# Fewer half slices beside the attention, three loads on ScalarE's queue, a shorter float64 conversion, and low weights on VectorE in every other step

## The chip, the cores and the metric

One core of one Trainium2 chip. The metric is device time in microseconds (us) of one launch. The tensor engine (TensorE, PE in the rows) multiplies; VectorE (DVE), ScalarE (ACT) and GpSimd (POOL) do elementwise work; SyncE (SP) issues most of the transfers (DMAs). Each engine works through its own instructions in order and waits on semaphores for the others. The kernel's matmuls are fp32, most of them as three products of a high and a low part.

## The reference

Three layers, one after the other, on 3072 tokens of 512 features:

```
state = gamma * state + k_t^T v_t;  y_t = scale * q_t state        # B=4, H=8, S=768, D=64
e = argmax(x w_gate); out = gate * sigmoid(x w_output_gate)[e] * relu(x w1[e]) w2[e]   # 8 experts, 512->1024->512
h = x w_in;  out = (h - tanh(h)) w_out                              # 512->2048->512
```

`w_in` and `w_out` come as float64; the kernel gets them as 64-bit words (`w64`) and makes two fp32 parts of each, high and low.

## The kernel before

The whole order of work is written out by hand; no scheduler moves anything.

**Attention** (`for n in range(NT - 1)`, lines 915 to 997). 24 tiles of 128 tokens, six for each batch element. A step loads a later tile (`load`, 1 MB of q, k, k, v), does `attend(n)` (state times q, state update, scores times v), `scores(n + 2)` (k times q, masked by VectorE into `pt`) and `rows(n)` (turns the tile, computes the gates' logits and stores the tokens to `xtok`). A tile's loads go five tiles ahead, later three. Six tile buffers are there up to step 18, then four. After 8, 16 and 24 tiles VectorE picks the expert of each token (`onehot`, `ranks`, `scale`, `slots`): the step's short VectorE instructions.

Beside it run half slices of the float64 weights. `load_m` brings one (128 x 512 words of 64 bits), `conv_m` makes its parts in three stages: `begin` (ScalarE), `v0` to `v5` (VectorE) and `high` (ScalarE), `rest` (GpSimd). For the last four slices of `w_in`/`w_out` (f of `NRES` and up) the parts stand in `keep` and `ta` and are stored to DRAM (`dh`, `dl`) until the dense layer; a later half slice takes the same `keep` buffer only when that store is done. `fill` gives VectorE instructions of `scales` and `convs` to a step until `MOST` = 2.6 us of estimated work are handed out; `pump` hands out those of ScalarE and GpSimd. At step `EARLIER` = 18 whatever is left of `convs` is issued at once, because its pool is given back.

**Experts** (`mm1`, `mm2`, lines 1001 to 1135). 72 steps of a 128-wide slice of one expert's hidden features: `mm1(i)` 12 matmuls, `mm2(i - 1)` 12 matmuls. `load_w` brings a slice (512 KB), `conv_w(i, 0)` and `conv_w(i, 1)` make its high part on ScalarE (line 236, `wh`) and its low part (line 238, `wl`): on GpSimd for part 0 (`mm1`'s weights), on VectorE for part 1 (`mm2`'s). Beside steps 14 to 66 the other 26 half slices are converted, one in two steps: stage 2 of one and stage 0 of the next in an even step, stage 1 in an odd one.

**Dense layer** (`mm3`, `mm4`, lines 1236 to 1262): six blocks of 512 tokens by 16 slices, 12 + 12 matmuls each.

What the change touches: `NPA`, `conv_w` (230), `conv_m` (263), `load` (589), the attention loop's loads and pieces (908 to 963), the end of the attention (1029 to 1042) and the loop over expert steps (1085 to 1126).

## Time and profile before

| | |
|---|---|
| time, median of 3 runs | 1042.34 us (1039.9 to 1042.95) |
| the profiled execution's own time | 1040.79 us |
| its span, first to last instruction | 1038.8 us |
| around the span | 2.0 us |
| busy in the span | PE 977.4, PE weight load 841.6, DVE 779.2, ACT 604.6, POOL 429.6 us |
| first matmul of the experts | 159.4 us |
| first matmul of the dense layer | 492.5 us |
| moved by DMA | 120.69 MB |

Times in rows are us from the start of the span. An instruction's row says its engine, line, operation and tiles (out<-in); in square brackets stands how long the engine was idle before it, and what ended that. The granted clock is TensorE's share of its full speed.

### The profile page before, as it was taken

What the parts mean: (1) busy time and instruction counts of PE and PEld (TensorE: products, weight loads), DVE (VectorE), ACT (ScalarE), POOL (GpSimd) and SP (SyncE); (2) the same over time, 40 slices, a digit from 0 to 9 for tenths busy, and PEclk for the clock granted to TensorE, in tenths of its full rate; (3) what the DMA queues carried; (4) which work ended last, traced back from release to release, by engine and by line L of the source; (5) the groups of instructions that cost most, each with busy time, mean ns of one, the idle gap of its engine ahead of it and who ended that gap; (6) DMA issues with size and microseconds to landing.
All of it is one profiled execution on the core that took longest, in us unless ns stands there. A gap on an engine that the chain in (4) does not pass through costs nothing.

```text
span 1038.8 us, 16501 instructions
## 1 busy us (share of the span) xinstructions
PE 977.4 (94%) x5938; PEld 841.6 (81%) x5938; DVE 779.2 (75%) x1183; ACT 604.6 (58%) x1090; POOL 429.6 (41%) x363
## 2 busy tenths in 40 slices
PE   7996676999999999999999999999999999999995
PEld 5875566999999999999888888888888888888884
DVE  2595765578989999994797777777777777777772
ACT  3433332265556565564786776677676667667662
POOL 4445341345645655644243352343324324323322
PEclk9998688999999999999999999999999999999998
DMA  9979361356757657664500010010001001000001
GB/s 333 345 280 362 127 208 62 112 190 208 213 163 244 202 179 232 199 189 154 204 21 21 1 61 11 11 41 22 19 11 52 11 11 51 11 0 21 21 1 43
DMA packets 44010, 120.69 MB, mean 116 GB/s; under 512 B 9638, under 2 KB 15014, under 8 KB 41106
## 3 DMA queue, kind: packets, MB, share of 16 engines
q1 hardware_dynamic: 35602, 100.38, 29.2%
q0 software_dynamic: 4864, 12.91, 3.8%
q10 hardware_dynamic: 3456, 6.29, 1.6%
q8 instruction: 48, 0.79, 0.3%
q14 instruction: 40, 0.33, 0.1%
HBM read 95.99 MB, written 23.57 MB: 115 GB/s over the span
## 4 chain that ended last, share of the span: by engine, by line
PE 66%; DVE 11%; DMA 10%; POOL 5%; issue 4%; ACT 2%; SPq 1%; POOLq 0%; ACTq 0%; DVEq 0%
PE mh L1194 26%; PE ma L1208 26%; PE ph L430 6%; PE ya L454 5%; DMA ld<-in_qkv 3%; POOL wl L238 3%; DMA wr<-in_w 2%; DVE wl L238 2%; DMA m<-in_w 1%; DVE ta L290 1%; ACT wh L236 1%; POOL ml L311 1%; DMA dh<-keep 1%; DVE ta L277 1%; DVE va L280 1%
## 5 line engine op out<-in xcount | busy, mean ns | idle before, releaser
L1176 POOL TENSOR_TENSOR gl<-g,gh 128x512 fp32r<-128x512 f32 x96 | 124.0, 1291 | 343.9 <-ACT gh L1175 327.6
L1194 PE MATMUL mh<-x2h,ml 128*128 128x512 f32 x384 | 151.7, 395 | 0.0
L1208 PE MATMUL ma<-ml,gh 128*128 128x512 f32 x384 | 151.6, 395 | 0.0
L1194 PE MATMUL mh<-x2h,mh 128*128 128x512 f32 x384 | 151.6, 395 | 0.0
L1208 PE MATMUL ma<-mh,gl 128*128 128x512 f32 x384 | 151.3, 394 | 0.0
L1208 PE MATMUL ma<-mh,gh 128*128 128x512 f32 x384 | 150.9, 393 | 0.0
L1194 PE MATMUL mh<-x2l,mh 128*128 128x512 f32 x384 | 150.9, 393 | 0.0
L1169 DVE COPY_PREDICATED g<-big,td 128x512 f32<-128x512 int32 x96 | 143.0, 1489 | 9.9
L1159 DVE SCALAR_TENSOR_TENSOR g<-s,mh 128x512 f32<-128x512 f32 x96 | 65.8, 686 | 101.8 <-ACT s L1157 87.1
L236 ACT ACTIVATE wh<-wr 128x512 fp32r<-128x512 f32 x136 | 84.3, 627 | 88.6 <-PE ya L454 75.9
L238 POOL TENSOR_TENSOR wl<-wr,wh 128x512 fp32r<-128x512 f32 x68 | 100.3, 1476 | 83.8 <-ACT wh L236 78.9
L1155 ACT ACTIVATE u<-mh 128x512 f32<-128x512 f32 x96 | 57.5, 599 | 128.2 <-PE mh L1194 123.6
L430 PE MATMUL ph<-xh,wl 128*128 128x216 f32 (+7 forms) x288 | 97.4, 338 | 5.9 <-POOL wl L238 5.5
L430 PE MATMUL ph<-xh,wh 128*128 128x216 f32 (+7 forms) x288 | 97.3, 338 | 0.1
L454 PE MATMUL ya<-lo,wh 128*128 128x216 f32 (+7 forms) x288 | 95.3, 331 | 0.7 <-DVE lo L434 0.7
L430 PE MATMUL ph<-xl,wh 128*128 128x216 f32 (+7 forms) x288 | 95.5, 332 | 0.3 <-DVE xl L410 0.3
L454 PE MATMUL ya<-hi,wh 128*128 128x216 f32 (+7 forms) x288 | 95.2, 331 | 0.0
L454 PE MATMUL ya<-hi,wl 128*128 128x216 f32 (+7 forms) x288 | 95.1, 330 | 0.0
L1194 PEld LDWEIGHTS mh<-x2l,mh 128*128 128x128 f32 x384 | 72.1, 188 | 17.2
L1194 PEld LDWEIGHTS mh<-x2h,ml 128*128 128x128 f32 x384 | 72.1, 188 | 17.2
L1208 PEld LDWEIGHTS ma<-mh,gh 128*128 128x128 f32 x384 | 72.1, 188 | 17.0
L1208 PEld LDWEIGHTS ma<-ml,gh 128*128 128x128 f32 x384 | 72.1, 188 | 17.0
(183 smaller groups left out, 2086.1 us busy)
## 6 DMA issues: line engine op xcount, KB each, us to landing
wr<-in_w SPq DMA_DIRECT2D x68, 512.0 KB, 5.2
ld<-in_qkv SPq DMA_DIRECT2D x22, 1024.0 KB, 13.5
m<-in_w SPq DMA_DIRECT2D x32, 512.0 KB, 5.0
xtok<-xr ACTq DMA_DIRECT2D x24, 256.0 KB, 7.4
...
```

Source lines behind the costliest of these rows:

```text
L236: nc.scalar.activation(hi, t[:, cs], AF.Copy)
L238: eng.tensor_tensor(out=lo, in0=t[:, cs], in1=f32(hi), op=ALU.subtract)
L277: V.tensor_scalar(mcv[j]["ta"], word(1), 5, 2, op0=ALU.logical_shift_left, op1=ALU.logical_shift_right)
L280: V.scalar_tensor_tensor(out=mcv[j]["va"], in0=word(1), scalar=0xC0000000, in1=mcv[j]["ta"], op0=ALU.bitwise_and, op1=ALU.bitwise_or,)
L430: nc.tensor.matmul(ph, a[:, cs], b[:, kk, 0:ns], start=(k == 0), stop=(k == 3 * KD - 1))
L454: nc.tensor.matmul(accs[p][dk], a[:, cs], b, start=(k == 0 and j == 0 and (p > 0 or dk % 2 == 0)), stop=(k == NFE - 1 and j == 2), skip_gr ...
L1155: nc.scalar.activation(u, h, AF.Square)
L1159: nc.vector.scalar_tensor_tensor(out=g, in0=s1, scalar=PB1, in1=h, op0=ALU.add, op1=ALU.mult)
L1169: nc.vector.copy_predicated(g, big.bitcast(I32), td)
L1176: nc.gpsimd.tensor_tensor(out=lo, in0=g, in1=f32(hi), op=ALU.subtract)
L1194: nc.tensor.matmul(h, a[:, cs], c, start=(k == 0), stop=(k == 3 * KD - 1))
L1208: nc.tensor.matmul(macc[b][t], a[:, cs], c[:, DM:2 * DM], start=(f == 0 and j == 0), stop=(f == NFM - 1 and j == 2))
```

## The change

1. `NPA` 6 to 4: two half slices less beside the attention (26 and 27 of 32), two more beside the experts. In the attention a further half slice is loaded only while fewer than two stand loaded and unused (`len(m64) < 2`).
2. `begin` multiplies the word by 2 to the minus 112 (`DOWN`) in place of squaring it (a copy with a scale); `v0` and `v1` read its result `keep`, not the word; `v5`, which zeroed tiny numbers, is gone.
3. Tile 2 is loaded ahead of `decay(2)` by SP, tiles 3 to 5 from ScalarE's queue.
4. The experts' first slices are loaded by `feed()` at the top of steps 15 and up, behind the tile's load, in place of `load_w()` at 13, 14, 15 and `feed()` at the end of a step.
5. At the end of the attention `run(sc[7:])` (17 short VectorE instructions) stands ahead of `mm1(2)`, and `slots` ahead of `conv_w(4, 1)`.
6. In the expert loop the low part 0 of odd steps is made by VectorE; that of even steps stays on GpSimd.
7. The 57 stages of the 28 remaining half slices are spread evenly over 53 steps.

```
@@ -53,7 +53,7 @@
 MOST = 2.6
 FAR = 1.0e6
 PG = P + 2 * E
-NPA = 6
+NPA = 4
 NRES = 12
 SCALE = 1.0 / float(D) ** 0.5
 
@@ -64,7 +64,8 @@
 PU = 0.36
 
 
-TINY = (1.125 * 2.0 ** -15) ** 2
+
+DOWN = 2.0 ** -112
 
 
 C_MASK = 0
@@ -227,14 +228,14 @@
         while state["load"] < min(len(loads), state["conv"] + 3):
             load_w()
 
-    def conv_w(i, part):
+    def conv_w(i, part, eng=None):
         t = raw[i]
         cs = slice(part * DM, (part + 1) * DM)
         pool = whl_p if i >= NFE or i % 4 < 2 else whl2_p
         hi = pool.tile([P, DM], F32R, tag=f"wh{part}", name=f"wh{part}_{i}", bufs=2)
         lo = pool.tile([P, DM], F32R, tag=f"wl{part}", name=f"wl{part}_{i}", bufs=2)
         nc.scalar.activation(hi, t[:, cs], AF.Copy)
-        eng = nc.vector if part else nc.gpsimd
+        eng = eng or (nc.vector if part else nc.gpsimd)
         eng.tensor_tensor(out=lo, in0=t[:, cs], in1=f32(hi), op=ALU.subtract)
         whl[i, part] = (hi, lo)
         if NFE // 2 <= i < NFE:
@@ -271,14 +272,14 @@
         def begin():
             t = {k: cv_p.tile([P, DM], U32, tag=k, name=f"{k}{j}", bufs=b) for k, b in cv_bufs[cv_p].items()}
             mcv[j] = t
-            nc.scalar.activation(f32(t["keep"]), f32(word(1)), AF.Square)
+            nc.scalar.activation(f32(t["keep"]), f32(word(1)), AF.Copy, scale=DOWN)
 
         def v0():
-            V.tensor_scalar(mcv[j]["ta"], word(1), 5, 2, op0=ALU.logical_shift_left, op1=ALU.logical_shift_right)
+            V.tensor_scalar(mcv[j]["ta"], mcv[j]["keep"], 4, 1, op0=ALU.logical_shift_left, op1=ALU.logical_shift_right)
 
         def v1():
             V.scalar_tensor_tensor(
-                out=mcv[j]["va"], in0=word(1), scalar=0xC0000000, in1=mcv[j]["ta"],
+                out=mcv[j]["va"], in0=mcv[j]["keep"], scalar=0x80000000, in1=mcv[j]["ta"],
                 op0=ALU.bitwise_and, op1=ALU.bitwise_or,
             )
 
@@ -293,10 +294,6 @@
         def v4():
             vf = f32(mcv[j]["va"])
             V.tensor_tensor(out=vf, in0=vf, in1=f32(mcv[j]["ta"]), op=ALU.add)
-
-        def v5():
-            vf = f32(mcv[j]["va"])
-            V.scalar_tensor_tensor(out=vf, in0=f32(mcv[j]["keep"]), scalar=TINY, in1=vf, op0=ALU.is_ge, op1=ALU.mult)
 
         def high():
             if f < NRES:
@@ -315,7 +312,7 @@
 
         return [
             [("A", begin), ("V", v0), ("V", v1), ("V", v2)],
-            [("V", v3), ("V", v4), ("V", v5)],
+            [("V", v3), ("V", v4)],
             [("A", high), ("P", rest)],
         ][stage]
 
@@ -586,7 +583,7 @@
                 cs = slice(hp * P, (hp + 1) * P)
                 nc.scalar.activation(qt[c][:, cs], qt[c - 1][:, cs], AF.Copy, scale=ca[:, C_STEP + hp:C_STEP + hp + 1])
 
-        def load(n):
+        def load(n, eng=nc.sync):
             if n < EARLIER and n % 6 >= 4:
                 t = ldb_p.tile([P, 4, DM], F32, tag="ld", name=f"ld{n}")
             else:
@@ -603,7 +600,7 @@
                 nc.sync.dma_start(t[:, 0:2], qkv[n, :, 0:2])
                 nc.sync.dma_start(t[:, 2:4], qkv[n, :, 2:4])
             else:
-                nc.sync.dma_start(t, qkv[n])
+                eng.dma_start(t, qkv[n])
             if n == 1:
                 nc.sync.dma_start(cb, conb)
                 nc.sync.dma_start(wgs, wg)
@@ -905,7 +902,9 @@
             nc.vector.tensor_copy(turn_rhs[:, kk, P:], wgs[:, kk])
         scores(1)
         nc.vector.tensor_copy(tri, cb[:, B_TRI:B_TRI + P])
-        nld = 2
+        load(2)
+        load(3, nc.scalar)
+        nld = 4
         decay(2)
         J0 = 2 * NFM - NPA
         convs, scales, soon, after = [], [], [], []
@@ -923,18 +922,18 @@
                 flush()
                 rooms()
             while nld < NT and nld <= n + (5 if nld < EARLIER + 4 else 3):
-                load(nld)
+                load(nld, nc.scalar if nld < 6 else nc.sync)
                 nld += 1
+            if n >= TA - 1:
+                feed()
             flush()
 
-            if n >= 2 and n % 2 == 0 and nload < NPA:
+            if n >= 2 and n % 2 == 0 and nload < NPA and len(m64) < 2:
                 load_m(J0 + nload, cva_p)
                 nload += 1
-            if n >= 4 and n % 2 == 0 and nconv < NPA:
+            if n >= 4 and n % 2 == 0 and nconv < nload:
                 convs += piece(J0 + nconv, cva_p)
                 nconv += 1
-            if n in (TA - 3, TA - 2, TA - 1):
-                load_w()
             if n == 6:
                 nc.gpsimd.tensor_copy(iota, ca[:, C_IOTA:C_IOTA + NS])
             if n > 0:
@@ -960,7 +959,6 @@
                 conv_w(q, 0)
             if 1 <= q < 5:
                 conv_w(q - 1, 1)
-                feed()
             cuts = [0, G - 3, G - 1] if final else [0, G]
             if g + 1 in cuts[1:]:
                 g0 = cuts[cuts.index(g + 1) - 1]
@@ -1031,13 +1029,13 @@
         nc.vector.tensor_scalar(first_idx, vc[:, :, 0], -float(P), 0.0, op0=ALU.add, op1=ALU.max)
         for c in chunks(1):
             gather(1, c)
+        run(sc[7:])
         mm1(2)
         conv_w(4, 0)
         mm2(1)
+        slots(gi, 0, G, 2 * E, NV)
         conv_w(4, 1)
         feed()
-        run(sc[7:])
-        slots(gi, 0, G, 2 * E, NV)
         nc.vector.tensor_tensor(out=first_s, in0=idxf[:, :, 3 * E:4 * E], in1=idxf[:, :, 4 * E:5 * E], op=ALU.add)
         nc.vector.tensor_tensor(out=first_s, in0=first_s, in1=idxf[:, :, 2 * E:3 * E], op=ALU.add)
         for i in range(3, NFE):
@@ -1085,13 +1083,26 @@
     NSTEP = len(steps)
     NPIECE = 2 * NFM - NPA
     CONV = NFE + NFE // 2 + 2
+    slots_m, nslot = [], 0
+    for j in range(NPIECE + 1):
+        ops = []
+        if j:
+            ops.append(lambda j=j: run(conv_m(j - 1, 2, cv_p)))
+        if j < NPIECE:
+            ops.append(lambda j=j: run(conv_m(j, 0, cv_p)))
+        slots_m.append(ops)
+        if j < NPIECE:
+            ops = [lambda j=j: run(conv_m(j, 1, cv_p))]
+            if j + 2 < NPIECE:
+                ops.append(lambda j=j: load_m(j + 2, cv_p))
+            slots_m.append(ops)
     for i in range(NFE, NSTEP + 1):
         p, k = divmod(i, NFE)
         feed()
         flush()
         nxt = i + 1 if i + 1 < NSTEP and i + 1 in loads else None
         if nxt:
-            conv_w(nxt, 0)
+            conv_w(nxt, 0, nc.vector if nxt % 2 else nc.gpsimd)
         if i < NSTEP:
             mm1(i)
         if i > NFE:
@@ -1114,16 +1125,11 @@
             cv_bufs[cv_p] = dict(keep=2, ta=2, va=2)
             load_m(0, cv_p)
             load_m(1, cv_p)
-        j = (i - CONV) // 2
-        if i >= CONV and i % 2 == 0:
-            if 1 <= j <= NPIECE:
-                run(conv_m(j - 1, 2, cv_p))
-            if j < NPIECE:
-                run(conv_m(j, 0, cv_p))
-        elif i >= CONV and j < NPIECE:
-            run(conv_m(j, 1, cv_p))
-            if j + 2 < NPIECE:
-                load_m(j + 2, cv_p)
+
+        while nslot < len(slots_m) and nslot * (NSTEP - NFE + 2 - CONV) < len(slots_m) * (i - CONV + 1):
+            for op in slots_m[nslot]:
+                op()
+            nslot += 1
         if i == NSTEP - NFE + 2:
             cv_p.release()
             for name in ("pk", "gx"):
```

Where ScalarE's and SP's instructions move at the end of the attention, and VectorE's beside the experts, their order shows it.

ScalarE, step 18 of the attention, before: `keep<-m` is `begin`, `keep<-va` is `high`, `wh` the high part of an expert's weights, `st` and `xT` belong to `attend(19)`.

```order
L722 ACTIVATE xr_1533<-tr_0_1534 128x256
L722 ACTIVATE xr_1533<-tr_1_1539 128x256
L727 DMA xtok<-xr_1533 128x512
L236 ACTIVATE wh_0_1545<-wr_1172 128x512
L306 ACTIVATE keep_1344<-va_1346 128x512
L274 ACTIVATE keep_1567<-m_31_1082 128x512
L306 ACTIVATE keep_1567<-va_1569 128x512
L687 ACTIVATE st<-up 128x256
L702 ACTIVATE xT_1624<-o_1606 128x512
L722 ACTIVATE xr_1645<-tr_0_1646 128x256
```

The same place now:

```order
L719 ACTIVATE xr_1517<-tr_0_1518 128x256
L719 ACTIVATE xr_1517<-tr_1_1523 128x256
L724 DMA xtok<-xr_1517 128x512
L237 ACTIVATE wh_0_1529<-wr_1304 128x512
L684 ACTIVATE st<-up 128x256
L699 ACTIVATE xT_1588<-o_1570 128x512
```

The two `high` and the `begin` that stood between `wh` and `st` are gone from here; the last of them now stands several steps earlier.

SP's queue from step 18 to step 20, before: `wr` is a slice of an expert, `ld` a tile of the attention, `dh` and `dl` a half slice's parts on their way to DRAM.

```order
L313 DMA dh_102<-keep_1344 128x512
L314 DMA dl_103<-ta_1345 128x512
L313 DMA dh_102<-keep_1567 128x512
L314 DMA dl_103<-ta_1568 128x512
L217 DMA wr_1665<-in_w 128x1024
L606 DMA ld_1680<-in_qkv 128x2048
L217 DMA wr_1749<-in_w 128x1024
L606 DMA ld_1751<-in_qkv 128x2048
```

Now, from step 15 on:

```order
L603 DMA ld_1302<-in_qkv 128x2048
L218 DMA wr_1304<-in_w 128x1024
L218 DMA wr_1306<-in_w 128x1024
L218 DMA wr_1308<-in_w 128x1024
L603 DMA ld_1375<-in_qkv 128x2048
L603 DMA ld_1642<-in_qkv 128x2048
L218 DMA wr_1644<-in_w 128x1024
L603 DMA ld_1713<-in_qkv 128x2048
L218 DMA wr_1715<-in_w 128x1024
```

The last two tiles' loads (`ld`) each stood behind a `wr`; now tile 22 (ld_1642) stands ahead of the fourth `wr`, tile 23 behind that one alone, and the stores have gone ahead.

VectorE beside expert steps 16 and 17, before: `ta` and `va` are `v0` to `v5` of a half slice, `lo` the low part of `mm1`'s result, `y` an expert's sums.

```order
L290 SCALAR_TENSOR_TENSOR ta_2844<-m_0_2735,ta_2844 128x512
L295 TENSOR_TENSOR va_2845<-va_2845,ta_2844 128x512
L299 SCALAR_TENSOR_TENSOR va_2845<-keep_2843,va_2845 128x512
L434 SCALAR_TENSOR_TENSOR lo_2928<-ph_2914,hi_2927 128x432
L463 COPY y_1_2946<-ya_1_2582 128x216
L463 COPY y_3_2952<-ya_3_2584 128x216
L238 TENSOR_TENSOR wl_17_2957<-wr_2788,wh_17_2956 128x512
L277 TENSOR_SCALAR ta_2965<-m_1_2737 128x512
L280 SCALAR_TENSOR_TENSOR va_2966<-m_1_2737,ta_2965 128x512
L286 TENSOR_SCALAR ta_2965<-va_2966 128x512
L434 SCALAR_TENSOR_TENSOR lo_2991<-ph_2977,hi_2990 128x432
L238 TENSOR_TENSOR wl_18_3011<-wr_2850,wh_18_3010 128x512
```

The same place now:

```order
L278 TENSOR_SCALAR ta_2874<-keep_2873 128x512
L281 SCALAR_TENSOR_TENSOR va_2875<-keep_2873,ta_2874 128x512
L287 TENSOR_SCALAR ta_2874<-va_2875 128x512
L239 TENSOR_TENSOR wl_17_2883<-wr_2752,wh_17_2882 128x512
L431 SCALAR_TENSOR_TENSOR lo_2900<-ph_2886,hi_2899 128x432
L460 COPY y_1_2918<-ya_1_2546 128x216
L460 COPY y_3_2924<-ya_3_2548 128x216
L239 TENSOR_TENSOR wl_17_2929<-wr_2752,wh_17_2928 128x512
L291 SCALAR_TENSOR_TENSOR ta_2874<-m_1_2701,ta_2874 128x512
L296 TENSOR_TENSOR va_2875<-va_2875,ta_2874 128x512
L431 SCALAR_TENSOR_TENSOR lo_2958<-ph_2944,hi_2957 128x432
L239 TENSOR_TENSOR wl_18_2978<-wr_2818,wh_18_2977 128x512
```

A second `wl_17` (part 0) stands ahead of `lo`, where `mm1(17)` waits for it; the instruction that read `keep` after `va` is gone, and `ta` and `va` now begin with `keep`.

## Rows read from the trace of the kernel before

**Rows 1.** Windows: busy us (x instructions) by engine, granted clock, DMA share, GB/s

```profile
core 0: us, PE busy (x) PEld busy (x) DVE busy (x) ACT busy (x) POOL busy (x), PEclk, DMA share, GB/s
18.40:94.00 75.60, 70.84 (x1121) 60.38 (x1122) 53.88 (x129) 31.00 (x77) 43.37 (x60) 1.00 0.85 327
94.00:128.00 34.00, 17.59 (x182) 15.18 (x184) 20.18 (x59) 9.77 (x24) 10.94 (x14) 0.65 0.55 218
128.00:159.40 31.40, 22.82 (x319) 19.65 (x315) 20.17 (x61) 10.56 (x23) 12.89 (x15) 0.89 0.54 182
163.40:170.80 7.40, 7.40 (x84) 7.26 (x84) 4.08 (x22) 2.59 (x9) 1.27 (x2) 1.00 0.11 39
177.05:188.70 11.65, 11.64 (x83) 11.58 (x83) 3.55 (x13) 2.68 (x6) 1.27 (x1) 0.60 0.21 63
300.00:400.00 100.00, 97.85 (x539) 93.93 (x538) 96.98 (x121) 58.43 (x108) 61.18 (x44) 1.00 0.67 209
513.00:1014.00 501.00, 501.00 (x2160) 405.51 (x2159) 381.83 (x458) 353.16 (x589) 178.23 (x132) 1.00 0.07 21
```

**Rows 2.** Timeline of PE, end of the attention and start of the experts

```profile
101.66 2.29 PE L719 MATMUL tr<-turn_rhs,xT 128*128 128x144 f32 x8 [6.48 <-ACT xT L702]
...
123.46 2.29 PE L719 MATMUL tr<-turn_rhs,xT 128*128 128x144 f32 x8 [8.79 <-ACT xT L702]
...
146.35 2.08 PE L634 MATMUL sc<-ld 64*128 64x128 f32 x16 [4.51 <-DMA ld<-in_qkv]
...
177.06 3.07 PE L862 MATMUL ip<-ohv,ohr 128*108 128x24 bf16 x32 [6.25 <-DVE ohv L849]
```

**Rows 3.** Timeline of ACT

```profile
27.80 0.87 ACT L722 ACTIVATE xr<-tr 128x256 f32<-128x256 f32 x2
...
99.13 0.67 ACT L274 ACTIVATE keep<-m 128x512 f32<-128x512 f32 x1 [8.82 <-DMA dh<-keep]
...
117.30 0.63 ACT L306 ACTIVATE keep<-va 128x512 fp32r<-128x512 f32 x1 [3.76 <-DVE va L299]
```

**Rows 4.** Timeline of SP's queue

```profile
85.71 0.33 SPq L260 DMA_DIRECT2D m<-in_w  x1
...
88.23 0.33 SPq L313 DMA_DIRECT2D dh<-keep  x1
...
129.13 0.33 SPq L217 DMA_DIRECT2D wr<-in_w  x1
```

**Rows 5.** Timeline of DVE

```profile
131.58 3.02 DVE L802 TENSOR_SCALAR ohr<-iota,rank 128x432 bf16<-128x432 f16 x8
...
168.75 0.17 DVE L1031 TENSOR_SCALAR first_idx<-v 108x4 int32<-108x4 f32 x1
...
170.92 3.71 DVE L238 TENSOR_TENSOR wl<-wr,wh 128x512 fp32r<-128x512 f32 x1 [0.65 <-ACT wh L236]
174.55 0.21 DVE L833 SCALAR_TENSOR_TENSOR den<-tau,den 128x64 f32<-128x64 f32 x1
```

**Rows 6.** Groups by line and shape: busy us, mean ns of one | idle before

```profile
L238 POOL TENSOR_TENSOR wl<-wr,wh 128x512 fp32r<-128x512 f32 x68 | 100.3, 1476 | 83.8 <-ACT wh L236 78.9 <-PE ph L430 4.6
...
L238 DVE TENSOR_TENSOR wl<-wr,wh 128x512 fp32r<-128x512 f32 x68 | 57.5, 846 | 19.5 <-ACT wh L236 18.6
...
L299 DVE SCALAR_TENSOR_TENSOR va<-keep,va 128x512 f32<-128x512 f32 x32 | 23.4, 730 | 1.0
```

**Rows 7.** Waits: engine, line and what it waited for, us, times, longest

```profile
PE ph L430 <- POOL wl L238: 5.5, 12, 0.9
```

**Rows 8.** Timeline of all engines, two pieces of the expert stage

```profile
338.15 1.48 POOL L238 TENSOR_TENSOR wl<-wr,wh 128x512 fp32r<-128x512 f32 x1
...
338.59 1.60 DVE L280 SCALAR_TENSOR_TENSOR va<-m,ta 128x512 uint32<-128x512 uint32 x1
...
347.76 0.50 ACT L433 ACTIVATE hi<-ph 128x400 fp32r<-128x400 f32 x1
...
349.87 0.40 PE L430 MATMUL ph<-xh,wl 128*128 128x400 f32 x1
...
350.15 0.70 DVE L280 SCALAR_TENSOR_TENSOR va<-m,ta 128x512 uint32<-128x512 uint32 x1
...
351.23 0.57 DVE L434 SCALAR_TENSOR_TENSOR lo<-ph,hi 128x400 fp32r<-128x400 f32 x1
```

More of the change, by code (lines that the diff above doesn't have):

```diff
@@ L55 @@
 PG = P + 2 * E
-NPA = 6
+NPA = 4
 NRES = 12
@@ L64 @@
 PU = 0.36
-TINY = (1.125 * 2.0 ** -15) ** 2
+DOWN = 2.0 ** -112
 C_MASK = 0
@@ L228, in feed, with conv_w @@
             load_w()
-    def conv_w(i, part):
+    def conv_w(i, part, eng=None):
         t = raw[i]
@@ L295, in v4 @@
             V.tensor_tensor(out=vf, in0=vf, in1=f32(mcv[j]["ta"]), op=ALU.add)
-        def v5():
-            vf = f32(mcv[j]["va"])
-            V.scalar_tensor_tensor(out=vf, in0=f32(mcv[j]["keep"]), scalar=TINY, in1=vf, op0=ALU.is_ge, op1=ALU.mult)
         def high():
@@ L907 @@
         nc.vector.tensor_copy(tri, cb[:, B_TRI:B_TRI + P])
-        nld = 2
+        load(2)
+        load(3, nc.scalar)
+        nld = 4
         decay(2)
@@ L1033 @@
             gather(1, c)
+        run(sc[7:])
         mm1(2)
@@ L1087 @@
     CONV = NFE + NFE // 2 + 2
+    slots_m, nslot = [], 0
+    for j in range(NPIECE + 1):
+        ops = []
+        if j:
+            ops.append(lambda j=j: run(conv_m(j - 1, 2, cv_p)))
+        if j < NPIECE:
+            ops.append(lambda j=j: run(conv_m(j, 0, cv_p)))
+        slots_m.append(ops)
+        if j < NPIECE:
+            ops = [lambda j=j: run(conv_m(j, 1, cv_p))]
+            if j + 2 < NPIECE:
+                ops.append(lambda j=j: load_m(j + 2, cv_p))
+            slots_m.append(ops)
     for i in range(NFE, NSTEP + 1):
@@ L1116 @@
             load_m(1, cv_p)
-        j = (i - CONV) // 2
-        if i >= CONV and i % 2 == 0:
-            if 1 <= j <= NPIECE:
-                run(conv_m(j - 1, 2, cv_p))
-            if j < NPIECE:
-                run(conv_m(j, 0, cv_p))
-        elif i >= CONV and j < NPIECE:
-            run(conv_m(j, 1, cv_p))
-            if j + 2 < NPIECE:
-                load_m(j + 2, cv_p)
+        while nslot < len(slots_m) and nslot * (NSTEP - NFE + 2 - CONV) < len(slots_m) * (i - CONV + 1):
+            for op in slots_m[nslot]:
+                op()
+            nslot += 1
         if i == NSTEP - NFE + 2:
```

30 lines of the change are left out of this document (14 added, 16 removed).

## The prediction

> **What bounds the kernel now.** I read the windows first [rows 1]. In the dense layer TensorE is busy 501 of 501 us: nothing hides there and nothing is to be won, so what the earlier stages lose or save reaches the end one for one. Between 300 and 400 us, among the experts, it is busy 97.85 of 100 and VectorE 96.98: two engines near their limit. The attention falls into two parts. From 18.4 to 94 us TensorE is busy 70.84 of 75.6 us at a granted clock of 1.00, while the DMA moves 327 GB/s. From 94 to 159.4 us it is busy only 17.59 + 22.82 = 40.4 of 65.4 us, and its instructions are slower: 182 take 17.59 us (97 ns each) and 319 take 22.82 us (72 ns), against 63 ns in the first part (70.84 us for 1121). The granted clock there is 0.65 and 0.89, a mixture of 1.2 and 2.4 GHz: after a long wait TensorE runs at the lower level for a while. So a stall costs its own length and some us behind it.
>
> TensorE's timeline says which stalls these are [rows 2]: 6.48 and 8.79 us until ScalarE's `xT`, 4.51 us until a tile's load, 6.25 us until VectorE's `ohv`. ScalarE's and SP's timelines give the causes. **First stall:** ScalarE stands 8.82 us in `begin` until a `dh` store has left the buffer `keep` [rows 3]; SP issued it only at 88.23, because it stood until 85.71 in a load of a half slice whose buffer was not free [rows 4]. **Second:** at step 18 the rest of the half slices is issued at once, and ScalarE, which must get past two `high`, waits at 117.30 for VectorE [rows 3] with `xT` behind it. **Third:** SP's load of the last tiles stands behind a `wr` that could go only at 129.13 [rows 4]. **Fourth:** the short VectorE instructions that end in `ohv` begin at 174.55, behind a `wl` that took 3.71 us [rows 5].
>
> **The change part by part.** The sum is made against the profiled execution, 1040.79 us (span 1038.8 and 2.0 around it); the median of the runs shown is 1.55 us above.
>
> *End of the attention (parts 1, 4 of the diff).* With four half slices for six, the wait on `dh` at 99 us falls on a half slice that no longer exists here, the burst at step 18 is empty, SP no longer stands in a half slice's load, and the last tiles' loads stand ahead of the `wr` that held them. All three stalls lose their cause. The 182 + 319 = 501 TensorE instructions at 63.2 ns are 31.7 us; idle time at the rate of the first part (4.76 us in 1121 instructions) adds 2.1: 33.8 us in place of 65.4, at most 31.6 us won. What is late next is VectorE: around step 19 eight `ohr` take 3.02 us [rows 5] and with a `wl` fill more than a step; TensorE also waits a little at each expert choice, and loads and stores now crowd into a shorter time. I leave 7.5 us for these, an estimate of about one us and a half for each of the five remaining steps, and book **-24.0**. The bounds are -31.6 and -13: at the lower gain one ScalarE wait of 8.8 us comes back with 2 us of lower clock behind it.
>
> *The tail (part 5).* The pair of windows before and after the fourth stall have nearly the same work: 84 instructions in 7.40 us, 83 in 11.64 [rows 1], 4.2 us lost to the clock, with 6.25 us of waiting 10.5 us. In the new order the short instructions begin when `first_idx` ends, at 168.75 + 0.17 = 168.92; they need the 2.5 us that they took from 174.55 until TensorE's wait ended at 177.06. That is 171.4, and TensorE arrives at 177.06 - 6.25 = 170.8. A wait of 0.6 us stays; with GpSimd's gathers beside it I say 1.5 and book **-9.0**. Bounds -10.5 and -4 (the short instructions take twice as long, and some of the clock is lost). The delayed `wl` is needed only two `mm2` later, and `lo` after twelve matmuls of `mm1(3)`, so both are covered.
>
> *First steps (parts 1, 3).* Of the 4.76 us that TensorE idles before 94 us, some belong to half slices on VectorE; two fewer of them, and `v5` gone, shorten that. Against it `begin` is now on VectorE's path: `v0` waits for ScalarE, and `load` instructions stand among ScalarE's. **-1.0**, bounds -3 and +4. The Trainium skill, "DMA: Bandwidth & Descriptors", section "Issuing engines are not separate DMA queues", says that a transfer started by another engine runs on the same 16 engines and saves only the time of issuing. By that rule issuing three tiles from ScalarE wins nothing by itself and this term is 0, by my reading of the rows -1.0; the first rows at 327 GB/s [rows 1] agree that the engines, not the queue, are near full.
>
> *Experts (parts 2, 6, 7).* TensorE waits 5.5 us in 12 pieces for GpSimd's low parts [rows 7]; that bounds the gain. VectorE's work: `v5` goes, 26 x 0.73 = -19.0 us; 30 low parts come, 30 x 0.846 = +25.4 [rows 6]; two more half slices come, each the five remaining instructions, about 5 us: +10. GpSimd gives up 30 x 1.476 = 44 us. Beside a GpSimd instruction a VectorE one is held: the same `va` takes 1.60 us at 338.59, beside GpSimd's `wl` of 338.15, and 0.70 at 350.15 [rows 8], 0.9 us lost. If each moved `wl` spares that once, 30 x 0.9 = -27. Together -19.0 + 25.4 + 10 - 27 = -11 us, so VectorE gets a little lighter, not heavier, and half of the 5.5 us should go: **-3.0**, bounds -5.5 and +8 (the 12 waits go, but each of the 30 moved low parts is waited for as long as those are now, 5.5 / 12 = 0.46 us: 13.8 - 5.5). The 28th half slice ends a step earlier than the 26th did, so the dense layer's loads from DRAM find their data; the dense layer itself: 0, covered by 501 of 501 us of matmuls.
>
> Sum: -24.0 - 9.0 - 1.0 - 3.0 = -37.0, 1040.79 - 37.0 = **1003.8, said as 1004 us**.
>
> **The rivals.** *A ScalarE wait comes back* (chance 0.17). `begin` of the third half slice still needs the first one's `dh` out of `keep`, now near step 8, in the part with 327 GB/s. If it waits 8.8 us as at 99.13, with 2 us of lower clock: 1015 us (1012 to 1022). For it: it is the same chain. Against it: the store is issued two steps earlier than its reader, as SP no longer stands in a load.
>
> *ScalarE's own stores fall behind its loads* (0.08). Three tiles are 3.1 MB; at 327 GB/s they need 9.6 us, and twice that beside SP's loads. Issued around 15 to 17 us they end between 25 and 35, and the first `xtok` store stands behind them. ScalarE's `xr` at 27.80, which waited for nothing before [rows 3], reuses that store's buffer and would wait up to 7 us, all of ScalarE behind it. With 2 us of clock: 1004 + 9 = 1013 us. The Trainium skill, same page, section "Queues, rings and completion order", has ScalarE's and SP's queues served in turn and each consumed in its order; by it this would happen. Against it: loads were ahead by several tiles, and SP has little left to send until 30 us.
>
> *VectorE becomes the bound among the experts* (0.05), the case on the other side. Today `lo` begins at 351.23, 3.47 us after `hi` at 347.76, while the second matmul of the next `mm1`, which needs the low part, starts at 349.87, 2.11 us after `hi` [rows 8]. The moved `wl` stands ahead of `lo`: in that place, with the 0.85 us of [rows 6], it ends 4.32 us after `hi`, so TensorE would wait 2.2 us. Over 30 steps 66 us; with three steps in four so late 50: 1004 + 3 + 50 = 1057 us. It decides from 40 / 30 = 1.3 us a step. Against it: a waiting TensorE lets VectorE catch up, and the sum above makes VectorE lighter.
>
> **How the numbers follow.** The forecast has 0.70, its own range 989 to 1012. Adding the two rivals of 1013 and 1015 carries the range to 1021, and the lower end is the sum with its terms near their better bounds (-31.6 - 10.5 - 3 - 5.5 = -50.6, 990): **989 to 1021**. A measurement of this kernel tells about 0.3%, 3 us, from no change. Slower by more needs the third rival nearly in full: 0.04; within 0.3%: 0.02; faster: 0.94.
>
> **What would show it.** In the changed profile the first `ph` should start near 134 us and the `ip` behind the tail wait under 2 us; the windows from step 18 on should show a granted clock near 1; TensorE's waits on `xT` should be gone from the top of the list; VectorE should be no busier per step among the experts, and TensorE's waits there under 5 us in all, on even steps. I am wrong if ScalarE still stands several us in a `keep`, if `xr` waits for `xtok` with TensorE behind it, if a new wait of TensorE for VectorE's `wl` adds up to more than 10 us, or if the dense layer starts later than 470 us.

## The result and the profile after

The changed kernel takes **1027.51 us** (median of 4 runs, 1026.86 to 1032.11) against 1041.87 us in the same session (4 runs, 1039.9 to 1042.95): a ratio of 0.9874, 95% interval 0.9841 to 0.9906. That is 1.3% faster, beyond the scatter of the runs, but 23.5 us slower than forecast and above the range given. The profiled execution took 1026.86 us, its span 1025.1 us instead of 1038.8.

Five stretches of the program, cut at TensorE's own instructions, show where the 13.7 us came from. They are read off TensorE's timeline of both kernels: the start of the scores of step 18, the first `ph`, the first `xt` of `turn(1)` behind it, the first `mh` of the dense layer, the end.

| stretch | before | after | difference | forecast |
|---|---|---|---|---|
| start to scores(18) | 94.02 | 99.85 | +5.8 | -1.0 |
| scores(18) to the first `ph` | 65.37 | 41.24 | -24.1 | -24.0 |
| first `ph` to `turn(1)`'s `xt` | 35.82 | 32.05 | -3.8 | -9.0 |
| that `xt` to the first `mh` | 297.49 | 305.37 | +7.9 | -3.0 |
| first `mh` to the end | 546.1 | 546.6 | +0.5 | 0 |

The windows of the changed kernel that answer to [rows 1], with some short ones behind the new stalls (columns as there):

```profile
core 0: us, PE busy (x) PEld busy (x) DVE busy (x) ACT busy (x) POOL busy (x), PEclk, DMA share, GB/s
18.25:99.85 81.60, 72.28 (x1121) 62.16 (x1121) 50.52 (x131) 32.22 (x79) 45.65 (x64) 0.96 0.92 335
24.00:30.00 6.00, 0.00 (x0) 0.00 (x0) 1.26 (x2) 0.86 (x3) 1.36 (x3) 0.80 0.88 311
30.00:36.00 6.00, 5.93 (x68) 5.15 (x70) 0.38 (x2) 2.88 (x10) 2.55 (x4) 0.63 0.56 213
99.85:141.09 41.24, 33.93 (x498) 29.11 (x496) 33.24 (x102) 16.78 (x39) 18.93 (x22) 0.96 0.58 206
151.00:156.00 5.00, 1.50 (x14) 1.37 (x13) 4.83 (x15) 1.91 (x4) 4.43 (x4) 1.00 0.34 90
156.00:161.00 5.00, 4.88 (x46) 4.88 (x46) 1.50 (x6) 0.00 (x1) 0.00 (x0) 0.63 0.20 36
161.00:166.00 5.00, 5.00 (x33) 4.94 (x33) 2.42 (x9) 2.05 (x5) 1.27 (x1) 0.69 0.51 177
300.00:400.00 100.00, 95.34 (x524) 90.64 (x523) 82.39 (x121) 57.74 (x107) 40.88 (x31) 1.00 0.64 204
```

The stalls of [rows 2] from step 18 on are gone, and that stretch runs at a granted clock of 0.96 in this execution (others are told further down). Three things are new. From 24 to 30 us TensorE does nothing, and the clock behind that is 0.63. At the tail it stands before 156 us, and the clock behind that is 0.63 and 0.69. Among the experts it is busy 95.34 of 100 us instead of 97.85, although VectorE, feared to be the bound there, has only 82.39 of work where it had 96.98. So that loss is not one of load.

**The start.** ScalarE's timeline of the changed kernel, TensorE's row that answers, and the `lead` rows on SyncE's queue:

```profile
13.73 0.41 ACTq L603 DMA_DIRECT2D ld<-in_qkv  x1
15.38 0.34 ACTq L603 DMA_DIRECT2D ld<-in_qkv  x1
15.76 0.72 ACTq L603 DMA_DIRECT2D ld<-in_qkv  x1
...
17.73 0.63 ACT L719 ACTIVATE xr<-tr 128x256 f32<-128x256 f32 x2
28.76 0.34 ACTq L724 DMA_DIRECT2D xtok<-xr  x1
29.14 0.39 ACT L684 ACTIVATE st<-up 128x256 f32<-128x256 f32 x1 [10.79 <-DMA x2c<-lead]
29.42 0.59 ACT L699 ACTIVATE xT<-o 128x512 f32<-128x512 f32 x1
```

```profile
30.07 2.29 PE L716 MATMUL tr<-turn_rhs,xT 128*128 128x144 f32 x8 [6.09 <-ACT xT L699]
```

```profile
14.13 8.90 SPq L611 DMA_DIRECT2D x2c<-lead  x4
```

The three loads leave at once. The first `xtok` store, ready at 18.36, leaves at 28.76, and `xT` with TensorE behind it stands until then. The row names as releaser a transfer that `st` doesn't read: the landing of a `lead` row, which SyncE issued from 14.13 on behind load 6.

**The tail.** VectorE's, GpSimd's and TensorE's rows there:

```profile
152.18 0.17 DVE L842 CAST part<-s 128x8 bf16<-128x8 f32 x1
...
152.25 1.00 POOL L376 DMA_INDIRECT gx<-xtok,first_idx  x1 [0.30 <-issue]
...
152.60 3.21 DVE L842 CAST part<-s 128x8 bf16<-128x8 f32 x1
153.28 2.48 POOL L239 TENSOR_TENSOR wl<-wr,wh 128x512 fp32r<-128x512 f32 x2
155.84 0.23 DVE L846 TENSOR_TENSOR ohv<-oh,part 128x64 bf16<-128x64 bf16 x1
156.12 2.06 PE L859 MATMUL ip<-ohv,ohr 128*108 128x24 bf16 x32 [3.61 <-DVE ohv L846]
```

The short instructions do come as early as forecast (the first of these casts at 151.72), but the last took 3.21 us where 0.17 is its time, until GpSimd's two subtractions end (153.28 + 2.48 = 155.76).

**Among the experts**, all engines of the changed kernel around one wait:

```profile
304.14 0.68 DVE L239 TENSOR_TENSOR wl<-wr,wh 128x512 fp32r<-128x512 f32 x1
...
304.30 0.67 ACT L275 ACTIVATE keep<-m 128x512 f32<-128x512 f32 x1
304.48 1.50 POOL L308 TENSOR_TENSOR ml<-va,mh 128x512 fp32r<-128x512 f32 x1 [1.65 <-ACT mh L303]
304.88 0.61 ACT L237 ACTIVATE wh<-wr 128x512 fp32r<-128x512 f32 x1
305.00 1.26 DVE L278 TENSOR_SCALAR ta<-keep 128x512 uint32<-128x512 uint32 x1 [0.18 <-ACT keep L275]
...
306.37 0.69 DVE L281 SCALAR_TENSOR_TENSOR va<-keep,ta 128x512 uint32<-128x512 uint32 x1
...
307.10 0.43 DVE L287 TENSOR_SCALAR ta<-va 128x512 uint32<-128x512 uint32 x1
307.44 0.68 DVE L239 TENSOR_TENSOR wl<-wr,wh 128x512 fp32r<-128x512 f32 x1
...
308.18 0.45 PE L427 MATMUL ph<-xh,wl 128*128 128x408 f32 x1 [1.59 <-DVE wl L239]
```

The high part `wh` is ready at 305.49, but its low part starts only at 307.44: ahead of it stand `v0` (1.26 us beside GpSimd's `ml`), `v1` and `v2` of slot A. The waits of the changed kernel in that stage (us in total, times, longest), where [rows 7] had one line of 5.5:

```profile
DVE ta L278 <- ACT keep L275: 18.1, 25, 1.3
...
PE ph L427 <- DVE wl L239: 7.9, 9, 2.0
...
PE ph L427 <- POOL wl L239: 2.5, 4, 1.2
```

### The profile page after: what moved, and what is told of

It is laid out like the page before. It is cut to its first block, busy times and chain, and to the rows that moved or that the text cites. A ratio compares the mean times of both kernels' runs of the same rounds, so it can differ in the third digit from the quotient of the medians.

```text
span 1025.1 us, 16478 instructions
## 1 busy us (share of the span) xinstructions
PE 972.1 (95%) x5938; PEld 837.6 (82%) x5938; DVE 744.6 (73%) x1181; ACT 604.0 (59%) x1090; POOL 379.1 (37%) x333
## 4 chain that ended last, share of the span: by engine, by line
PE 78%; DVE 9%; issue 4%; DMA 4%; ACT 2%; POOL 2%; SPq 0%; ACTq 0%; POOLq 0%; DVEq 0%
PE mh L1200 26%; PE ma L1214 26%; PE ph L427 9%; PE ya L451 9%; PE tr L716 2%; PE sc L631 1%; DMA x2c<-lead 1%; DVE ta L278 1%; DVE va L281 1%; PE o L690 1%; DVE wl L239 1%; DMA xtok<-xr 1%; DVE pt L624 1%; POOL wl L239 1%; DMA ld<-in_qkv 1%
## 5 line engine op out<-in xcount | busy, mean ns | idle before, releaser
L1165 DVE SCALAR_TENSOR_TENSOR g<-s,mh 128x512 f32<-128x512 f32 x96 | 65.8, 686 | 101.6 <-ACT s L1163 86.9
L239 DVE TENSOR_TENSOR wl<-wr,wh 128x512 fp32r<-128x512 f32 x98 | 71.5, 731 | 34.2 <-ACT wh L237 33.5
```

What stands on the lines that cost most here:

```text
L239: eng.tensor_tensor(out=lo, in0=t[:, cs], in1=f32(hi), op=ALU.subtract)
L1165: nc.vector.scalar_tensor_tensor(out=g, in0=s1, scalar=PB1, in1=h, op0=ALU.add, op1=ALU.mult)
```

## The experiments

All start from the changed kernel but one, which starts from the kernel before. The table has the median of each and its stretches in the one profiled execution that each run has. The times of one kernel's runs scatter by up to 13 us from lowest to highest, and the kernel before had medians of 1039.75 to 1041.87 us in the four sessions, so the stretches carry the reading. Ratios are to the kernel before in the same session.

The stretches scatter too, and the table shows by how much. Six of its programs are the same, instruction for instruction, up to the first `ph`: the changed kernel, the tail's low parts on VectorE, all low parts on GpSimd, part 0 a step earlier, part 0 ahead of the slots, `begin` early. In them scores(18) start between 99.1 and 102.3 us, and the stretch from there to the first `ph` takes 41.2 to 47.2 us, at granted clocks from 0.96 to 0.86. The changed kernel's own profile is one of the two shortest. From the first `ph` to `xt` the five of them that are still the same take 30.4 to 33.7 us.

| run | median us | scores(18) at | first `ph` at | to `xt` | to `mh` |
|---|---|---|---|---|---|
| kernel before | 1041.87 | 94.0 | 159.4 | 35.8 | 297.5 |
| changed kernel | 1027.51 | 99.8 | 141.1 | 32.05 | 305.4 |
| loads on SyncE | 1022.92 | 91.1 | 138.3 | 32.05 | 305.4 |
| lead rows late | 1027.37 | 96.2 | 143.4 | 33.1 | 305.4 |
| before, loads on ScalarE | 1046.82 | 101.7 | 164.8 | 33.9 | 296.6 |
| tail's low parts on VectorE | 1023.07 | 102.3 | 146.6 | 25.8 | 305.4 |
| all low parts on GpSimd | 1024.53 | 99.7 | 140.9 | 30.4 | 297.6 |
| part 0 a step earlier | 1048.47 | 99.1 | 146.4 | 33.7 | 321.2 |
| part 0 ahead of the slots | 1023.01 | 101.6 | 145.8 | 30.4 | 296.9 |
| `begin` early | 1026.92 | 99.3 | 143.5 | 32.05 | 303.8 |
| three repairs | 1011.50 | 92.5 | 136.5 | 25.8 | 303.2 |
| the same, GpSimd's low parts | 1011.55 | 95.5 | 140.0 | 25.8 | 299.1 |
| three repairs, marks spread | 1010.03 | 92.4 | 137.2 | 27.0 | 298.2 |
| the same, low parts on VectorE | 1011.65 | 95.8 | 143.6 | 27.0 | 298.3 |

### The start: loads on SyncE

```
-        load(3, nc.scalar)
+        load(3)
...
-                load(nld, nc.scalar if nld < 6 else nc.sync)
+                load(nld)
```

> The changed kernel with loads 3 to 5 on SyncE's queue again, all else kept. Theory A (the 5.8 us lost between the start and scores(18) come from ScalarE, which stands 10.4 us at the issue of its first xtok store): the store is issued near 18.5 us and not at 28.8, TensorE's wait of tr for xT (6.8 us) falls under 1.5 us, scores(18) start at 94 to 96 us and not at 99.9, and the whole is 4 to 6 us shorter than the changed kernel, 1021 to 1024 us. Theory B (the time is lost to what the loads bring and when, not to the engine that issues them: load 6 and the lead rows share the transfers' time with loads 3 to 5): the store goes early but sc then waits for its loads instead, scores(18) stay at 98 to 100 us and the whole at 1026 to 1028 us.

1022.92 us (ratio to before 0.9831, 0.9797 to 0.9865). The store leaves at 17.52 and no wait for `xT` above 0.7 us is left; scores(18) start at 91.1, 8.7 us earlier and better than expected: theory A holds, B falls. At the first `ph` only 2.8 of the 8.7 us are left. It looks as if the end of the attention gave the rest back. The stretch from scores(18) to there, in this run:

```profile
91.10:138.30 47.20, 38.76 (x499) 33.31 (x497) 33.77 (x105) 16.77 (x39) 18.37 (x22) 0.86 0.52 184
```

The matmuls take 38.76 us at 0.86 where they took 33.93 at 0.96, 4.8 of the 6 us. TensorE's waits there are 2.3 us for `cnt`, where the changed kernel has 1.2, and the same 3.7 us for `pt`. But the run with part 0 a step earlier, whose start is the changed kernel's (scores(18) at 99.1), has the same stretch to 0.02 us:

```profile
99.13:146.35 47.22, 38.76 (x499) 33.45 (x497) 33.85 (x105) 16.78 (x39) 18.37 (x22) 0.86 0.52 182
```

So the lower clock comes without the repaired start too, and is not shown to be its price. Over the six programs with the old start scores(18) begin at 100.3 us and the first `ph` at 144.0 in the mean; over the three with this repair and the same attention otherwise (this one, the three repairs, and those with GpSimd's low parts) at 93.0 and 138.3. Of 7.3 us gained at scores(18) 5.8 are left at the first `ph`; the 1.5 us between are within the scatter.

### The start: lead rows late

```
-            if n == NCH:
+            if n == 2 * NCH:
                 for kk in range(KD):
                     nc.sync.dma_start(x2c[kk, :, 0:PRE], lead)
```

> The changed kernel with its loads on ScalarE as they are, and only the four lead rows (x2c) and the far tokens written later, with load 12 and not with load 6. Theory A1 (in the compiled program each transfer signals one of eight semaphores, given out in turn, and is issued only when the transfer that had it before has landed; the first xtok store has that of the first lead row, and that row lands behind load 6): with the lead rows gone from there the store follows load 2, is issued between 18.3 and 20 us, tr's wait for xT falls under 2 us, and the whole is 3 to 6 us shorter than the changed kernel. Theory A2 (three loads of 1 MB outstanding on ScalarE's own queue hold up the issue of the next transfer on it): the store is still issued at 27 to 29 us, tr still waits 5 us or more, and the whole stays within 1.5 us of 1027.5 us.

1027.37 us (0.9871, 0.9836 to 0.9906). ScalarE's timeline in this run:

```profile
19.86 0.34 ACTq L724 DMA_DIRECT2D xtok<-xr  x1
...
33.27 0.66 ACT L719 ACTIVATE xr<-tr 128x256 f32<-128x256 f32 x2 [2.82 <-DMA xtok<-xr]
```

The store leaves at 19.86 with all three loads still issued on ScalarE ahead of it. So it is not the outstanding loads that hold an issue up (A2 falls): the store waited for the lead row. `tr`'s longest wait for `xT` fell to 1.5 us, also as A1 has it; only its 3 to 6 us for the whole missed. ScalarE now waits 2.82 us at 33.27 because the first store lands late behind the loads on its own queue, which is the rival "ScalarE's own stores fall behind its loads", seen where the longer wait no longer hides it. scores(18) regain 3.6 us; the stretch behind them takes 47.2 us, which the old start shows too, so this run's first `ph` at 143.4 tells neither way.

### The start: the kernel before, with part 3 alone

```
-        nld = 2
+        load(2)
+        load(3, nc.scalar)
+        nld = 4
...
-                load(nld)
+                load(nld, nc.scalar if nld < 6 else nc.sync)
```

> The kernel before with part 3 of the change alone: loads 3 to 5 on ScalarE's queue. Theory A1 (the first xtok store then waits for the first lead row): the store is issued at 27 to 30 us, tr waits 5 to 7 us for xT, scores(4) start at 33 to 37 us and not at 25.9, and scores(18) 5 to 9 us later than 94.0. What reaches the end: by the mirror run (loads on SyncE in the changed kernel: 8.7 us regained at scores(18), 2.8 us left at the first ph), 2 to 5 us, 1043 to 1047 us. If the end of the attention here is set by VectorE's backlog alone (theory H), scores(18) are late but the first ph stays within 1 us of 159.4 and the whole within 1.5 us of 1041 us.

1046.82 us, ratio 1.0057 (1.0034 to 1.008): part 3 alone makes the kernel before 0.6% slower. The store leaves at 27.44, `tr` waits 6.1 us, scores(18) start 7.7 us late. Theory A1 holds, H falls: the first `ph` is 5.4 us late, and the median 5.7 us higher. Most of what the start loses reaches the end.

### The tail: two low parts on VectorE

```
-        conv_w(4, 0)
+        conv_w(4, 0, nc.vector)
...
-                conv_w(i + 2, 0)
+                conv_w(i + 2, 0, nc.vector if i == 3 else nc.gpsimd)
```

> The changed kernel with the part 0 low parts of steps 4 and 5, the two that GpSimd runs behind the first gathers, on VectorE instead. Theory F (VectorE's cast of 128x8, 0.2 us elsewhere, took 3.21 us from 152.60 to 155.81 because GpSimd held something it needs through its gather and its two subtractions, which end at 155.76): the cast takes under 1.3 us, ip's wait for ohv falls from 3.6 to under 1.5 us, and the stretch from the first ph to turn(1)'s xt takes 29 to 31 us and not 32.05. Rival G (the cast's record is late for another reason, and the chain behind slots() sets the tail): the cast or ip's wait stays as long, and the stretch at 31.5 to 33 us. The whole is 1 to 3 us shorter by F, within 1 us by G: too little for three rounds to tell, so the trace is to decide.

The three casts in this run, and what TensorE waits for (timeline of all engines):

```profile
156.40 1.03 POOL L376 DMA_INDIRECT gx<-xtok,first_idx  x1 [16.86 <-DVE ex L831]
...
157.19 0.21 DVE L842 CAST part<-gates 128x8 bf16<-128x8 f32 x1
157.66 0.17 DVE L842 CAST part<-s 128x8 bf16<-128x8 f32 x1
157.74 1.00 POOL L376 DMA_INDIRECT gx<-xtok,first_idx  x1 [0.30 <-issue]
...
158.07 0.17 DVE L842 CAST part<-s 128x8 bf16<-128x8 f32 x1
...
158.55 0.62 PE L859 MATMUL ip<-ohv,ohr 128*108 128x24 bf16 x10 [0.57 <-DVE ohv L846]
```

And its windows behind that wait:

```profile
156.00:161.00 5.00, 4.42 (x58) 4.29 (x58) 3.91 (x22) 1.91 (x4) 2.03 (x2) 1.00 0.31 92
161.00:166.00 5.00, 5.00 (x47) 4.98 (x46) 4.54 (x14) 2.78 (x6) 1.28 (x1) 1.00 0.58 175
```

F holds, G falls. The gathers don't hold the casts; the two subtractions did. The wait shrinks by 3.0 us and the stretch by 6.3, because the granted clock stays at 1.00: the other 3.3 us were what the stall cost behind itself in that execution. The wait is 3.61 us in all seven profiles with the changed kernel's tail and 0.53 to 0.57 in the five with the repaired one; the stretch is 30.4 to 33.7 us in the seven, 25.8 to 27.0 in the five. So 3.0 us of the gain are the wait, and what comes on top varies from under half a us to 5. The whole, 1023.07 us (ratio 0.9821, 0.9782 to 0.9859), is 4.4 us below the changed kernel's median, which is from another session.

### The experts: all low parts on GpSimd

```
-            conv_w(nxt, 0, nc.vector if nxt % 2 else nc.gpsimd)
+            conv_w(nxt, 0)
```

> The changed kernel with the part 0 low parts of all steps on GpSimd again (part 6 undone). If moving them to VectorE was the loss among the experts (theory E), the stage from turn(1)'s xt to the first mh takes 297 to 301 us and the whole is 4 to 7 us shorter than the changed kernel. By theory C the cause is where slot A stands and waits, not the engine of the low part: GpSimd then holds its low part and the conversion's subtraction together, v0 to v4 grow back towards the 1.0 to 1.25 us each that they took before, PE waits 5 to 10 us for GpSimd's wl, and the whole lies within 3 us of the changed kernel, on either side.

1024.53 us (0.9866, 0.9832 to 0.99); the stage takes 297.6 us, so read by theory E part 6 costs 7.8 us. Its profiled execution is the fastest of its four runs (1017.21). TensorE waits 5.2 us for GpSimd's `wl`, as before the change [rows 7], which is C's sign. E and C part at the next run but one.

### The experts: part 0 a step earlier

```
-        if nxt:
-            conv_w(nxt, 0, nc.vector if nxt % 2 else nc.gpsimd)
         if i < NSTEP:
             mm1(i)
+        nx2 = i + 2
+        if nx2 < NSTEP and nx2 in loads:
+            conv_w(nx2, 0, nc.vector if nx2 % 2 else nc.gpsimd)
```

> The changed kernel with the expert weights' part 0 (high on ScalarE, low on VectorE or GpSimd as before) issued one step earlier, behind mm1(i) and ahead of the conversion's half steps. Theory C (order: in odd steps the low part stands on VectorE behind v0 to v2, which wait for begin and for GpSimd's subtraction, and TensorE waits for it; the engine has time enough): PE's waits for wl, 10.4 us on both engines in the changed kernel, fall under 3 us, the stage from turn(1)'s xt to the first mh takes 298 to 301 us and not 305.4, and the whole is 4 to 7 us shorter. Theory D (load: the low parts, the conversion and GpSimd's blocking add up to too much for VectorE whatever their order): the waits move to lo or to the part 1 low parts, the stage stays at 303 to 306 us and the whole within 2 us of 1027.5 us.

1048.47 us: slower than both kernels (1.0074, 1.0044 to 1.0104). It tells nothing of C or D, for a reason not thought of: ScalarE now asks for each slice before it has come. Its line in this run's list of waits:

```profile
ACT wh L237 <- DMA wr<-in_w: 64.4, 27, 5.7
```

In the stage of the changed kernel the same wait is 4.6 us. ScalarE stands in it with `hi`, `begin` and `xh` behind it.

### The experts: part 0 ahead of the slots

```
-        if nxt:
-            conv_w(nxt, 0, nc.vector if nxt % 2 else nc.gpsimd)
...
+        nx2 = i + 2
+        if nx2 < NSTEP and nx2 in loads:
+            conv_w(nx2, 0, nc.vector if nx2 % 2 else nc.gpsimd)
```

> The changed kernel with one reordering among the experts: the next step's part 0 (high on ScalarE; low on VectorE in odd steps, on GpSimd in even ones, as in the change) is issued ahead of the conversion's half steps of the step before instead of behind them. No load is needed earlier than before. Theory C (place: on VectorE the odd steps' low part loses because it stands behind v0 to v2 and their wait for begin): PE's waits for VectorE's wl, 7.9 us, fall under 2 us, the stage from turn(1)'s xt to the first mh takes 297 to 300 us and not 305.4, as with all low parts on GpSimd (297.6), and the whole is 4 to 8 us shorter than the changed kernel, 1020 to 1023 us. Theory E (VectorE is the wrong engine for them wherever they stand: its rate or its load): waits of another tile on VectorE (lo, part 1's wl, xl) take their place, and the stage stays at 303 to 306 us.

1023.01 us (0.9833, 0.9784 to 0.9882), the stage 296.9 us. The waits of TensorE in this run's stage:

```profile
PE ph L427 <- DVE xl L407: 2.7, 1, 2.7
PE ya L451 <- DVE lo L431: 2.6, 3, 1.4
PE ph L427 <- POOL wl L239: 2.3, 3, 0.9
```

The wait for VectorE's `wl` is gone with VectorE still making 30 of them. Place was the cause, C; E falls. The changed kernel's order takes 305.4 us in all four profiles that have it; this order takes 296.9 here and 298.2 to 303.2 in the three runs further down that share it. `v0` still waits 19.4 us for `begin`, and that costs TensorE nothing now.

### The experts: `begin` early

Stage 4 of `conv_m` is `begin` alone, now issued in slot B of the half slice before; slot A keeps `v0` to `v2`, which are stage 3.

```
-            ops.append(lambda j=j: run(conv_m(j, 0, cv_p)))
+            ops.append(lambda j=j: run(conv_m(j, 3 if j else 0, cv_p)))
...
+            if j + 1 < NPIECE:
+                ops.append(lambda j=j: run(conv_m(j + 1, 4, cv_p)))
```

> The changed kernel with begin(j+1) issued in slot B of half slice j and no longer in slot A right ahead of v0, all else kept: v0 then waits for nothing, and starts ahead of GpSimd's subtraction of the half slice before. Theory C1 (what is late is VectorE's chain behind v0's wait, 18.1 us in 25 waits, and v0's 1.01 us beside GpSimd where 0.43 is its time alone): v0's wait falls under 3 us, PE's waits for VectorE's wl from 7.9 to 2 to 5 us, the stage takes 299 to 303 us, the whole 2 to 6 us less than the changed kernel. Theory C2 (the mere 1.5 to 2.5 us of slot A's operations ahead of the low part are enough): v0's wait goes but PE's waits for wl stay at 6 us or more and the stage at 303 us or more.

1026.92 us (0.9857, 0.9813 to 0.9901), the stage 303.8 us. `v0`'s wait is gone altogether and TensorE's for VectorE's `wl` falls to 3.1 us, as C1 had it; but its wait for GpSimd's `wl` grows from 2.5 to 7.6 us, and the stage gains 1.6 us, as C2 had it. The wait changed engines; what holds GpSimd was not followed up.

### Together: three repairs

Loads on SyncE, the tail's two low parts on VectorE, part 0 ahead of the slots.

> The changed kernel with three of the repairs together: loads 3 to 5 on SyncE, the low parts of steps 4 and 5 on VectorE in the tail, and the next step's part 0 ahead of the conversion's half steps among the experts. If the three causes are separate and each is what the single runs showed: first ph near 138.3 us (as with the loads on SyncE), 25.8 us to turn(1)'s xt, 296.9 us to the first mh and 546.5 us to the end, a span near 1007.5 us and a median of 1006 to 1013 us, below both kernels. If VectorE's backlog at the end of the attention takes back what the start regains, the first ph stays at 141 to 146 us and the median at 1011 to 1018 us.

**1011.5 us, ratio 0.9709 (0.9678 to 0.974)**: below both kernels. Start and tail do what they did alone (first `ph` at 136.5, 25.8 us). The expert stage takes 303.2 us, not 296.9: its matmuls are busy 293.06 us instead of 289.27, with a clock of 0.91 between 400 and 440 us, and one wait of 1.6 us for ScalarE's `wh` is new. The two runs with the marks spread have the same instructions there and take 298.2 and 298.3 us.

### Together: GpSimd's low parts in place of the reordering

> As the run with three repairs, but with the experts' part 0 low parts all on GpSimd in the changed kernel's order (part 6 undone) instead of the reordering. By theory C the engine hardly matters once the odd steps' low part doesn't stand behind slot A: the stage from turn(1)'s xt to the first mh takes 297 to 299 us, and the whole lies within 2 us of the run with three repairs. If VectorE's lower load is worth something of its own, it is 3 us or more behind it.

1011.55 us (0.9707, 0.9667 to 0.9746), the stage 299.1 us: the engine hardly matters, as C has it.

### Together: the marks spread

```
-                    later.append(("V", mark))
+                    later.append(("V", mark, 0.5))
```

> The three repairs, and the planner's cost of one mark (the 128x432 comparison on VectorE) 0.5 us instead of the 0.2 it is put down for (0.33 us each alone, 0.54 us beside GpSimd), so that eight of them no longer stand in one step ahead of pt. Theory J (the 3.66 us wait of sc for pt near step 20, in every kernel with the changed attention, comes from those eight marks in a row, 4.32 us; and the granted clock of 0.50 that follows it goes with it): that wait falls under 1.5 us, the clock stays at 1.00 between steps 20 and 23, scores(20) to scores(23) take 18 to 21 us and not 24.5, and the whole is 3 to 6 us shorter than with the three repairs. If VectorE's sum of work is what binds there, the wait moves to another step, the stretch keeps its length within 1.5 us, and the whole stays within 1.5 us.

1010.03 us (0.9698, 0.9671 to 0.9725), 1.5 us below the three repairs and within their scatter (1007.41 to 1014.93), where 3 to 6 were expected. The longest wait for `pt` falls from 3.65 to 1.6 us, and the 15.1 us from scores(20) to scores(23) (21.5 with the three repairs) run at a clock of 1.00:

```profile
102.50:117.60 15.10, 14.20 (x219) 11.83 (x217) 14.93 (x37) 8.15 (x20) 13.03 (x16) 1.00 0.78 257
...
124.00:130.00 6.00, 4.58 (x36) 3.83 (x32) 2.37 (x10) 1.73 (x4) 2.06 (x2) 0.50 0.51 164
130.00:137.20 7.20, 4.73 (x41) 3.68 (x41) 3.65 (x14) 1.07 (x3) 0.00 (x0) 0.50 0.10 38
```

So the marks were that stall. But the first `ph` doesn't come earlier. The first gathers, issued at 123.80 and 125.30, are late next: TensorE waits 2.88 us for their `gx` until 132.47. The lower level of the clock, 0.50, is granted from 124 us on, ahead of that wait; what brought it there isn't shown. The 19.6 us from scores(23) to `ph` (10.4 with the three repairs) take the 6.4 us back and more.

### Together: low parts of the attention's end on VectorE

```
-                conv_w(q, 0)
+                conv_w(q, 0, nc.vector)
```

> As the run before, and the low parts of the attention's last conversions (steps 0 to 3, part 0) on VectorE instead of GpSimd. There GpSimd holds VectorE's short operations up (0.5 to 0.95 us where 0.2 is theirs alone) while it runs those low parts: if that blocking outweighs the 4 times 0.7 us that VectorE gets to do, the attention's end is 1 to 3 us earlier than in the run before; if VectorE's sum binds, it is up to 3 us later.

1011.65 us (0.9707, 0.968 to 0.9733): within the scatter of the run before. Its profile has the first `ph` 6.4 us later, but 3.5 us of that are there at scores(18), ahead of the edit. It settles nothing.

## Why the prediction was right and wrong

**End of the attention, -24.0: the mechanism held, the number in part by luck.** The three stalls lost their cause as argued; that parts 1 and 4 did it is read from the traces, as no run undoes them alone. The stretch fell by 24.1 us in the one profile of the changed kernel. The five other programs with the same instructions there fell by 18.2 to 24.1, 21.2 in the middle. The 7.5 us left for "what is late next" are 7.4 in that profile and up to 13.4 in the others. The sum took the matmuls at 63.2 ns throughout, 31.7 us, and had no term for a lower clock; in these profiles they take 33.9 to 38.8 us. What is late is what was named, the eight `ohr`, and behind them the gathers.

**First steps, -1.0, between -3 and +4: +5.8.** The step that failed is the sentence that "`load` instructions stand among ScalarE's" at no price of their own. Issuing them is cheap (0.34 to 0.72 us each). What it missed is that moving them off SyncE moves load 6 and the four lead rows forward, past the store in the compiled order of all transfers, and that the store then waits for a lead row. The rival had ScalarE, the place and the engine right, and an amount of 9 us where 5.8 were lost; its cause, the buffer of `xr`, shows only with the lead rows away. The sentence on order of queues (the Trainium skill, "DMA: Bandwidth & Descriptors", section "Queues, rings and completion order") fits what was seen there: behind three loads on its queue the store of 19.86 landed only at about 33, when `xr` could go on.

**The tail, -9.0: -3.8, and -8.8 to -10.0 once repaired.** The order, the arrival of TensorE and the 0.6 us of wait left over were right to 0.1 us in the repaired run. The failed step took the 3.71 us of `wl` in [rows 5] for that instruction's own slowness, and thought it moved out of the way. It was the sign that GpSimd held VectorE at that time, and the new order put the cast there. The row was read and the neighbour not; in the kernel before, GpSimd's two subtractions end at 174.07, and that `wl` at 174.63:

```profile
171.59 2.48 POOL L238 TENSOR_TENSOR wl<-wr,wh 128x512 fp32r<-128x512 f32 x2
```

The Trainium skill, "SBUF — State Buffer", section "Who interferes with whom", states that VectorE and GpSimd share a pair of ports, that a cast can need it, and that the one which comes second is blocked for the other's whole instruction. The trace agrees on the blocking: the cast's end at 155.81 lies 0.05 us behind the subtractions' end at 155.76. On who came second it doesn't: by its row the cast began before them (GpSimd's spans are rough).

**Experts, -3.0: +7.9, near the bound of +8.** VectorE did get lighter, and by more than the 11 us worked out: 232.8 us in the stage, where it was 257.6. The failed step is "and half of the 5.5 us should go", which made a wait out of a load: TensorE's waits for low parts are 10.4 us (7.9 and 2.5) instead. The third rival priced the place of the moved `wl`, but only as ahead of `lo`. It also stands behind `v0` to `v2`, as the order printed ahead of the prediction shows, and `v0` behind `begin`, a wait that the prediction named for the first steps and not here. Even in the right place no profile has the stage clearly shorter than before the change (296.9 to 303.2 against 297.5); what eats the rest, the two half slices more or something else, no run tells. Parts 2 and 7 were not run alone.

**Dense layer, 0: +0.5**, as forecast. Of the signs named beforehand, "the dense layer starts later than 470 us" came true (478.5), and the new wait for VectorE's `wl` stayed below its 10 us with 7.9. The first `ph` near 134 us (141.1) and the tail's wait under 2 us (3.61) did not come. Of the rivals none came as written.

The forecast's 1004 us was thus not far from what the idea can do: with its three misplaced pieces put right it gives 1010 to 1011.7 us, inside the range.
